# Keys asked for on another queue, and the opening split by heads: one change to a chunked delta rule with a maxout layer

## The chip, the cores and the metric

The kernel runs on one core of a Trainium2 chip. The time is device microseconds of one launch. Five engines work side by side, each on its own list of instructions in order: TensorE (PE in the profile; PEld is its loading of the stationary operand), VectorE (DVE), ScalarE (ACT), GpSimd (POOL) and SyncE (SP), which here only issues DMA transfers. POOL issues some too. An engine that reaches an instruction whose operand is not ready stands, and all behind it stand with it.

## The reference

Two parts, the second fed by the first. The first is a delta rule: for each of 4 batches and 8 heads a 48 x 48 state runs over 768 tokens.

```
k_n = k / (norm(k) + 1e-6)
for t in range(S):
    y[:, :, t] = q[:, :, t] @ state
    v_old = state^T k_t
    state = state + beta_t * outer(k_t, v_t - v_old)
x = y.transpose(0, 2, 1, 3).reshape(3072, 384)
```

The second is a maxout layer: `h = max(x @ w1, x @ w2, x @ w3)`, then `out = h @ w_out`, with w1 to w3 of 384 x 768 and w_out of 768 x 384. All operands are float32; the weights come as 64-bit floats, so that the kernel reads them as pairs of 32-bit words and puts float32 together itself.

## The kernel before, in words

**Tiles.** The 768 tokens are cut into 12 chunks of 64. A unit is one chunk for two of the four batches (one in each half of the 128 partitions), so chunk c has the units 2c and 2c + 1. Four units, that is two chunks, are a group, numbered m from 0; the third group has units 8 to 11 and chunks 4 and 5. `load_k(n)` and `load_q(n)` (L128 and L131; their transfers are issued in the helper `load`, L118) fetch a unit's keys and queries by two DMA transfers of 96 KB each; the keys of units 8 to 11 go into the buffers `kpad` that units 0 to 3 have used. `load_v(c)` fetches a chunk's values.

**What is made of a chunk.** Keys and queries are transposed by PE into `p_t` and copied to `kqt` (`turn`, L342 to L364). Gram products go into `p_g` (`gram`, L435): keys with keys give `at`, keys with queries give `pt`, masked on VectorE (L419). Within a chunk the delta rule needs the inverse of a triangular matrix. Its diagonal blocks are solved by column steps on VectorE (`solve`, the pairs L562 and L566), for a whole group at once; group 0's blocks return straight from VectorE's transpose to the tiles `ut` (L570 to L583), those of later groups go through DRAM (`y_d`, L588 and L597). For the first two groups (chunks 0 to 3) the solved blocks have 16 rows, and `halves_z` (PE `p_e`, copied to `zs`, L671 and L674), `halves_t` (VectorE transposes, L643 and L645) and `halves_u` (PE `p_f`, negated into `ut`, L678 and L680) join them to 32. Then `join_z` (`p_z`, L705 to L710), `turn_t1` (transposes L629 and L631) and `join_u` (`p_j`, negated, L719) join 32 to 64. With the inverse, `old_k` takes the state's part off the values (`p_k`), `new` makes u (`p_u`, copied at L769), `step` adds to the state (`p_s`, L787 and L794), `to_y` gives y (`p_y`, L806 to L810) and `to_x` transposes y into x (`p_x`, L820, copied at L870 to L873).

For chunk 0 `heads_of` cuts the heads into two halves of four, with a copy engine for each: ScalarE for the first, VectorE for the second. For later chunks there is one piece of eight heads, with ScalarE. Before the change `halves_u` and `join_u` do not use that engine: `negated` (L676) goes by `bb`, the half of the partitions.

**Norms and values.** `prep_values(c)` scales a chunk's values by the keys' norms on POOL (`scale`, L284), if that has not been done yet.

**Weights.** `fetch` (L213) asks for a piece of 384 KB on SP, into one of five buffers. A step of `weights` (called `conv`) scales a piece on ScalarE (L232, L233) and joins the piece before it, on VectorE (L243, L247) and POOL (L251). There are 24 pieces.

**The maxout layer.** `ffn(m)` treats the 512 tokens of group m. Each of its steps i is three matmuls into `p_h` (L922) in one of two PSUM banks, and a copy or maximum to `h`; at the end come four products into `p_o` (L954).

**Order.** The order of all instructions is written by hand; nothing is moved by a scheduler. The opening (chunk 0 and the start of chunk 1) is a straight list of calls from L990 to the start of `ffn(0)`. From there on the loop over the steps i of `ffn(0)` places the rest: `FIRST` (chunk 1 and the queries of group 0), `EARLY_LINKS` (chunks 2 and 3, and the transposes t and Gram products g of units 8 to 11: t0 stands at i = 11), and lines of its own for loads, weight steps and solving steps. Later groups go by `LINKS` in `ffn(1)` and on; there `p` means `prep_values`, and p1 stands at i = 5. The lines that matter here:

```
        if 7 <= i < 11:
            load_k(i + 1)
...
        if i in (22, 25):
            prep_values(4 + i // 25)
```

`load_k` without a second argument goes to SP's queue.

Of the kernel before, what the change touches and what calls it, by code (L numbers as in the profile page):

```python
# [21 lines left out]
def kernel(  # L22
# [495 lines left out]
    def solve(m):  # L518


        x = in_rows(xs[m])
        if m == 1:
            y_bl = in_wo(1)
        else:
            y_bl = work.tile([128, 2, HB * BL + HB], FP32, name="y_bl", bufs=1)
            if m:
                zero = kpad[0][:, 0:1, D : D + 1]
                nc.scalar.copy(y_bl, zero.to_broadcast(y_bl.shape))
            else:
                nc.gpsimd.memset(y_bl, 0.0)  # L530
        y = in_rows(y_bl)
        bl = small("bl", BL)
        norm(bl, diagonal(x), small("root_bl", BL), small("nt_bl", BL))
        if m:
            norms_of(m, bl)
        nc.vector.reciprocal(bl, bl)
        nc.vector.tensor_tensor(out=bl, in0=bl, in1=bl, op=ALU.mult)
        nc.vector.tensor_tensor(out=bl, in0=bl, in1=beta_bl[:, m] if m else beta_0, op=ALU.mult)
        (nc.scalar.copy if m else nc.gpsimd.tensor_copy)(diagonal(y), bl)
        if m < FINE:  # L540
            size, xv, yv = HB, in_blocks(xs[m]), in_blocks(y_bl)
            xb = xv[:, :, :, 0:HB]
            by = bl.rearrange("p (s i) -> p s i", i=HB)[:, :, None, :]
            by = by.to_broadcast([128, 2, HB, HB])
        else:
            size, xv, yv = BL, x[:, None], y[:, None]
            xb, by = x, bl[:, None, :].to_broadcast([128, BL, BL])
        nc.vector.tensor_tensor(out=xb, in0=xb, in1=by, op=ALU.mult)
        yield
        for j in range(size - 1):  # L550
            a, b = j + 1, size - 1 - j
            n = BL // size
            tmp = work.tile([128, 256], FP32, name="tmp")
            t_v = tmp[:, 0 : n * a * b].rearrange("p (s c i) -> p s c i", s=n, i=b)
            row, column, rest = (
                xv[:, :, j, None, j + 1 : size],
                yv[:, :, 0:a, j, None],
                yv[:, :, 0:a, j + 1 : size],
            )
            if n == 1:  # L560
                row, column, rest, t_v = (t[:, 0] for t in (row, column, rest, t_v))
            nc.vector.tensor_tensor(  # L562
                out=t_v, in0=row.to_broadcast(t_v.shape),
                in1=column.to_broadcast(t_v.shape), op=ALU.mult,
            )
            nc.vector.tensor_tensor(out=rest, in0=rest, in1=t_v, op=ALU.subtract)  # L566
            yield
        if m == 0:
            back = in_rows(xs[0])
            nc.vector.transpose(out=back, in_=y.rearrange("p c i -> p i c"))  # L570
            yield
            for cc in range(2):
                for i in range(4):
                    bb, half = divmod(i, 2)
                    r = block(bb, half)
                    to = ut[cc][r, :, :, BL * half : BL * (half + 1)].rearrange(
                        "p g h i -> p (g h) i"
                    )
                    of = back[r, :, 16 * cc : 16 * (cc + 1)].rearrange("p i x -> p x i")
                    if half:  # L580
                        nc.scalar.copy(to, of)
                    else:
                        (nc.gpsimd if cc else nc.vector).tensor_copy(to, of)  # L583
                yield
            return
        y_d = dram.tile([2, 2, B, H, BL, BL], FP32, name="y_d")
        for cc in range(2):
            nc.sync.dma_start(  # L588
                out=y_d[cc].rearrange("f b h i j -> (f b h) i j"),
                in_=y[64 * cc : 64 * (cc + 1)],  # L590
            )
        yield
        for cc in range(2):
            for half in range(2):
                for bb in range(2):
                    r0 = C * bb + BL * half
                    (one_queue if m or cc else both_queues)[bb].dma_start(  # L597
                        out=ut[cc][
                            r0 : r0 + BL, :, :, BL * half : BL * (half + 1)
                        ].rearrange("p g h i -> p (g h) i"),  # L600
                        in_=y_d[cc, half, 2 * bb : 2 * bb + 2].rearrange(
                            "b h c i -> c (b h) i"
                        ),
                    )
            yield
# [53 lines left out]
    def span(hs):  # L659
        return slice(hs[0], hs[-1] + 1)  # L660

    def halves_z(c):
        if c > 1:
            halves_t(c)
        at = [ats[2 * c + g] for g in range(2)]
        second = ut[c % NU].rearrange("p g h (f two x) -> p g h f two x", two=2, x=HB)
        for hs, p_v, copy in heads_of(c, "p_e", BL):
            for i, h in enumerate(hs):
                for bb, g in TILES:
                    r = rows(bb)  # L670
                    nc.tensor.matmul(  # L671
                        p_v[rows(bb ^ g), g, i], at[g][r, h], second[r, g, h, :, 1]
                    )
            copy(zs[c % NU][:, :, span(hs)], p_v)  # L674

    def negated(bb, to, of, c=0):  # L676
        if bb and c < 2:
            nc.vector.tensor_scalar_mul(to, of, -1.0)  # L678
        else:
            nc.scalar.mul(to, of, -1.0)  # L680

    def halves_u(c):
        t, z = fine.pop(c), zs[c % NU]
        for hs, p_v, _ in heads_of(c, "p_f", BL):
            for i, h in enumerate(hs):
                for bb, g in TILES:
                    r = rows(bb ^ g)
                    nc.tensor.matmul(p_v[rows(bb), g, i], t[g][r, h], z[r, g, h])
            for f in (0, 1):
                for bb in range(2):  # L690
                    r = block(bb, f, HB)
                    negated(
                        bb,
                        ut[c % NU][r, :, span(hs), BL * f + HB : BL * (f + 1)],
                        p_v[r, :, :, HB * f : HB * (f + 1)],
                    )

    def join_z(c):
        at = [ats.pop(2 * c + g) for g in range(2)]
        z, second = zs[c % NU], ut[c % NU][:, :, :, BL:C]  # L700
        for hs, p_v, _ in heads_of(c, "p_z", BL):
            for i, h in enumerate(hs):
                for bb, g in TILES:
# [1 line left out]
                    nc.tensor.matmul(  # L705
                        p_v[block(bb ^ g), g, i], at[g][r, h, 0:BL], second[r, g, h]
                    )
            nc.scalar.copy(z[block(0), :, span(hs)], p_v[block(0)])
            copy = nc.vector.tensor_copy if c < 2 else nc.scalar.copy
            copy(z[block(1), :, span(hs)], p_v[block(1)])  # L710

    def join_u(c):
        z, t = zs[c % NU], t1[c % NU]
        u12 = ut[c % NU][:, :, :, BL:C]
        for hs, p_v, _ in heads_of(c, "p_j", BL):
            for i, h in enumerate(hs):
                for bb, g in TILES:
                    r = block(bb ^ g)
                    nc.tensor.matmul(p_v[block(bb), g, i], t[r, g, h], z[r, g, h])  # L719
            for bb in range(2):  # L720
                negated(bb, u12[block(bb), :, span(hs)], p_v[block(bb)], c)


    xts, rhss, qss, us, yts = {}, {}, {}, {}, {}
# [33 lines left out]
    def new(c):  # L758
        rhs = rhss.pop(c)
        u = us[c] = both("u", D, 2)  # L760
        for hs, p_v, copy in heads_of(c, "p_u", D):
            for i, h in enumerate(hs):
                for bb, g in TILES:
# [3 lines left out]
                        rhs[rows(bb), g, h],  # L767
                    )
            copy(u[:, :, span(hs)], p_v)  # L769
        if c + NU < 2 * FINE:  # L770
            for bb in range(2):
                corner = ut[c % NU][block(bb), :, :, BL:C]
# [39 lines left out]
    def to_x(c):  # L812
# [1 line left out]
        if m not in xts:  # L814
            xts[m] = work.tile([128, KT, TOK], FP32, name="xt")
        y_f = yts.pop(c).rearrange("p g h d -> p g (h d)")
        p_x = ps_two("p_x")
        for g in range(2):
            for t in range(KT):
                nc.tensor.transpose(  # L820
                    p_x[:, g, t * 128 : (t + 1) * 128],
                    y_f[:, g, t::KT],
                    ident,
                )
        xt = xts[m][:, :, cc * 256 : (cc + 1) * 256].rearrange(
            "p t (g x) -> p g t x", g=2
        )
        copied(c, xt, p_x[:, :, 0 : KT * 128].rearrange("p g (t x) -> p g t x", t=KT))

    yds, yqs = {}, {}  # L830

# [24 lines left out]
    def turn_y(c):  # L856
# [6 lines left out]
            ),  # L863
            in_=yqs.pop(c).rearrange("p b (x t) -> p b t x", t=KT),
        )

    def copied(c, to, of):

        if c:
            nc.scalar.copy(to, of)  # L870
        else:
            nc.scalar.copy(to[:, 0], of[:, 0])
            nc.vector.tensor_copy(to[:, 1], of[:, 1])  # L873


    def less_first(f):
        part = (slice(None), slice(None), slice(f * 128, (f + 1) * 128))
# [167 lines left out]
        scale(c, nrm_0[:, c])  # L1045
    some(conv, 1)
    halves_u(0)
    turn_t1(0)
    join_z(0)
    masked(pts[0], by_par(pts[0]))  # L1050
    join_u(0)
    masked(pts[1], by_par(pts[1]))
    old_k(0)
    old_q(0)
    some(solving, 1)
    new(0)
    some(conv, 1)
    fetch(nc.sync)
    to_y(0)
    some(conv, 1)  # L1060
    fetch(nc.sync)
    halves_z(1)
    to_x(0)
    some(conv, 1)
    fetch(nc.sync)
    halves_t(1)
    load_q(4)
    load_v(2)
# [58 lines left out]
    for i, _ in enumerate(ffn(0)):  # L1127
# [7 lines left out]
            some(solving, (4, 2, 1)[i - 4])  # L1135
        if i in (5, 7):
            prep_values(i // 2)
        if 7 <= i < 11:
            load_k(i + 1)
        if i == 0:  # L1140
            load_v(3)
        if i == 12:
            load_q(11)
        if i in (10, 18):
# [3 lines left out]
        if i == 21:  # L1148
            solving = solve(2)
            some(solving, 1)  # L1150
        if i in (22, 25):
            prep_values(4 + i // 25)
        if 21 < i < 27:
            some(solving, 3)
        if i >= 27:
# [55 lines left out]
```

## Time and profile before

| what | value |
|---|---|
| median of 4 runs | 546.33 us (541.83 to 548.56) |
| the profiled execution | 546.7 us, span 545.0 us |
| PE busy | 507.4 us, 93% |
| DVE busy | 315.7 us, 58% |
| ACT busy | 155.3 us, 28% |
| POOL busy | 167.0 us, 31% |
| granted TensorE clock, mean | 0.952 |
| DMA | 53.49 MB, mean 98 GB/s |
| instruction queue | 63 packets, 1.03 MB |

The span is cut into 40 equal slices of 13.6 us; the page gives for each the busy share in tenths and, as PEclk, the clock that TensorE was granted in tenths of full speed:

```profile
PE   8558898889979999999998999999999999999996
...
PEclk9855799979989999999999999999999999999999
DMA  8872747973213494434375546483323401130011
```

From the thirteenth slice on PE is at 9 nearly throughout. What is below lies in the first twelve slices, up to 163 us; the clock is at a half in slices 3 and 4 (27 to 54 us), and for a part of several others up to slice 12.

"Issue" as the reason of a wait is time in which the engine waited for nothing that the profile shows. A wait for several events is put down to the last.

### The profile page before, as it was taken

What the parts mean: (1) busy time and instruction counts of PE and PEld (TensorE: products, weight loads), DVE (VectorE), ACT (ScalarE), POOL (GpSimd) and SP (SyncE); (2) the same over time, 40 slices, a digit from 0 to 9 for tenths busy, and PEclk for the clock granted to TensorE, in tenths of its full rate; (3) what the DMA queues carried; (4) which work ended last, traced back from release to release, by engine and by line L of the source; (5) the groups of instructions that cost most, each with busy time, mean ns of one, the idle gap of its engine ahead of it and who ended that gap; (6) DMA issues with size and microseconds to landing.
All of it is one profiled execution on the core that took longest, in us unless ns stands there. A gap on an engine that the chain in (4) does not pass through costs nothing.

```text
span 545.0 us, 18537 instructions
## 1 busy us (share of the span) xinstructions
PE 507.4 (93%) x8096; PEld 314.9 (58%) x8096; DVE 315.7 (58%) x701; ACT 155.3 (28%) x285; POOL 167.0 (31%) x279
## 2 busy tenths in 40 slices
PE   8558898889979999999998999999999999999996
PEld 7446677766535655556555556565565555654453
DVE  5886988665898544179854388671989313101100
ACT  4536364457310324220124210143201231010100
POOL 6315025122276073477065567141330000000000
PEclk9855799979989999999999999999999999999999
DMA  8872747973213494434375546483323401130011
GB/s 109 185 163 73 153 112 172 181 185 80 70 31 85 105 196 74 105 96 125 91 160 111 114 118 148 104 139 87 86 68 82 79 2 53 52 72 1 0 22 36
DMA packets 118848, 53.49 MB, mean 98 GB/s; under 512 B 100976, under 2 KB 113456, under 8 KB 118768
## 3 DMA queue, kind: packets, MB, share of 16 engines
q1 hardware_dynamic: 109872, 40.01, 33.9%
q0 software_dynamic: 6784, 11.92, 9.4%
q8 instruction: 63, 1.03, 0.8%
q10 hardware_dynamic: 2112, 0.39, 0.5%
q14 instruction: 17, 0.14, 0.1%
HBM read 39.17 MB, written 13.11 MB: 96 GB/s over the span
## 4 chain that ended last, share of the span: by engine, by line
PE 80%; DVE 11%; issue 3%; ACT 2%; DMA 2%; SPq 1%; POOL 0%; DVEq 0%; ACTq 0%; POOLq 0%
PE p_h L922 35%; PE p_o L954 24%; PE p_g L435 4%; PE p_m L902 2%; PE p_y L806 2%; PE p_k L736 2%; PE p_u L764 2%; DVE tmp L562 2%; DMA kpad<-in_k_dram 2%; PE p_j L719 2%; PE p_t L358 2%; PE p_q L736 1%; PE p_z L705 1%; PE p_s L787 1%; DVE y_bl L566 1%
## 5 line engine op out<-in xcount | busy, mean ns | idle before, releaser
L922 PE MATMUL p_h<-xt,w_sb 128*128 128x512 f32 (+1 forms) x522 | 222.9, 572 | 7.0 <-DVE h L936 3.6
L922 PEld LDWEIGHTS p_h<-xt,w_sb 128*128 128x128 f32 x522 | 98.0, 197 | 95.4 <-issue 88.4
L954 PE MATMUL p_o<-wo_sb,h 128*128 128x384 f32 x288 | 97.8, 489 | 0.0
L936 DVE TENSOR_TENSOR h<-h,p_h 128x512 f32<-128x512 f32 (+1 forms) x48 | 29.7, 618 | 96.6 <-PE p_h L922 96.5
L954 PEld LDWEIGHTS p_o<-wo_sb,h 128*128 128x128 f32 x288 | 53.7, 190 | 35.7 <-issue 0.5
L562 DVE TENSOR_TENSOR tmp<-x_bl,y_bl 128x31 f32<-128x31 f32 (+20 forms) x139 | 49.9, 359 | 4.1
L566 DVE TENSOR_TENSOR y_bl<-y_bl,tmp 128x31 f32<-128x31 f32 (+20 forms) x139 | 49.2, 354 | 4.8
L960 ACT COPY o_sb<-p_o 128x384 f32<-128x384 f32 x24 | 11.5, 480 | 141.7 <-PE p_o L954 135.7
L932 ACT ACTIVATE h<-p_h 128x512 f32<-128x512 f32 x30 | 17.9, 597 | 87.4 <-PE p_h L922 83.0
L954 PE MATMUL p_o<-w_sb,xt 128*128 128x384 f32 x120 | 42.0, 486 | 0.0
L393 POOL DMA_DIRECT2D turned<-in_q_dram x72 | 39.2, 552 | 3.1 <-POOL turned L388 3.1
L435 PE MATMUL p_g<-kqt 48*64 48x64 f32 (+1 forms) x1216 | 30.0, 246 | 10.8 <-ACT kqt L364 5.5
L251 POOL TENSOR_TENSOR w_sb<-mant,up 128x384 int32<-128x384 int32 x18 | 18.0, 999 | 59.5 <-DVE mant L247 51.0
L435 PEld LDWEIGHTS p_g<-kqt 48*64 48x64 f32 x1216 | 25.7, 145 | 18.1 <-issue 8.1
L954 PEld LDWEIGHTS p_o<-w_sb,xt 128*128 128x128 f32 x120 | 22.8, 190 | 15.9
L419 DVE TENSOR_TENSOR pt<-p_g,mask 128x512 f32<-128x512 f32 x22 | 15.2, 691 | 23.9 <-PE p_g L435 23.8
L284 POOL TENSOR_TENSOR v_t<-v_t,nrm 128x768 f32<-128x768 f32 x12 | 17.9, 1492 | 26.5 <-DVE nrm L263 13.5
L794 DVE TENSOR_TENSOR st<-st,p_s 48x768 f32<-48x768 f32 (+1 forms) x18 | 17.1, 951 | 15.0 <-PE p_s L787 14.8
L137 POOL DMA_DIRECT2D v_t<-in_v_dram x12 | 9.9, 830 | 38.9 <-PE p_u L764 38.9
L388 POOL MEMSET turned<- 128x96 f32 x18 | 3.3, 193 | 54.9 <-DVE kqt L409 34.7
L118 POOL DMA_DIRECT2D kpad<-in_k_dram x24 | 16.3, 688 | 11.5 <-PE p_s L787 11.5
L452 ACT COPY at<-p_g 128x512 f32<-128x512 f32 x21 | 12.3, 586 | 23.6 <-DVE pt L419 21.7
(150 smaller groups left out, 610.3 us busy)
## 6 DMA issues: line engine op xcount, KB each, us to landing
w_bits<-in_moe_w_dram SPq DMA_DIRECT2D x18, 384.0 KB, 4.8
out_dram<-o_sb SPq DMA_DIRECT2D x48, 96.0 KB, 2.2
turned<-in_q_dram POOLq DMA_DIRECT2D x72, 48.0 KB, 2.6
y_x<-y SPq DMA_DIRECT2D x16, 192.0 KB
qall<-y_x SPq DMA_DIRECT2D x32, 96.0 KB, 3.0
at_d<-at SPq DMA_DIRECT2D x80, 32.0 KB, 1.9
ut<-y_d SPq DMA_DIRECT2D x40, 64.0 KB, 2.7
qall<-in_q_dram SPq DMA_DIRECT2D x24, 96.0 KB, 4.2
```

Source lines behind the costliest of these rows:

```text
L251: nc.gpsimd.tensor_tensor(out=dst.bitcast(I32), in0=mant_v.bitcast(I32), in1=up_v, op=ALU.add)
L284: nc.gpsimd.tensor_tensor(out=vts[c], in0=vts[c], in1=nrm[:, :, :, None].to_broadcast([128, 2, H, D]), op=ALU.mult,)
L393: (queue, nc.gpsimd)[i].dma_start(out=t[p0 : p0 + 32, bb, at : at + NP * 2 * D].rearrange("p (j x) -> p j x", j=NP), in_=(k, q)[i][2 * bb ...
L435: nc.tensor.matmul(p_g[rows(bb ^ (g * i)), par, c0 : c0 + C * (1 + whole)], kq[:, 0], kq if whole else kq[:, i],)
L562: nc.vector.tensor_tensor(out=t_v, in0=row.to_broadcast(t_v.shape), in1=column.to_broadcast(t_v.shape), op=ALU.mult,)
L566: nc.vector.tensor_tensor(out=rest, in0=rest, in1=t_v, op=ALU.subtract)
L736: nc.tensor.matmul(p_b[rows(bb), par, c0 : c0 + D], kqt[g][dims(par), j, bb ^ g, i], st[dims(par), bb ^ g, g, j],)
L794: nc.vector.tensor_tensor(out=s_v[r], in0=s_v[r], in1=p_s[r, :, 0 : H * D], op=ALU.add)
L922: nc.tensor.matmul(p_h, w_sb[i][:, t, f * 128 : (f + 1) * 128], xt[:, t, lo : lo + w], start=(t == 0), stop=(t == KT - 1),)
L932: nc.scalar.activation(out=h, in_=p_h, func=mybir.ActivationFunctionType.Relu)
L936: nc.vector.tensor_tensor(out=h, in0=h, in1=p_h, op=ALU.max)
L954: nc.tensor.matmul(p_o, stays, moves, start=(n == 0), stop=(n == len(terms) - 1))
```

## The change

1. The keys of units 8 to 11. Before, `load_k(i + 1)` for 7 <= i < 11 on SP's queue. Now POOL issues units 8 and 9 at i = 1 and units 10 and 11 at i = 7.
2. The opening. In `solve`, of the four copies to chunk 0's `ut` three are VectorE's and one is ScalarE's (two and two before), and chunk 1's first-half copies go from POOL to VectorE. `halves_z` of chunk 0 copies both halves of the heads on ScalarE. `negated` takes the engine that `heads_of` gives: for chunk 0 ScalarE for the first four heads and VectorE for the last four, for later chunks ScalarE alone. `join_z` copies on ScalarE alone, also for chunks 0 and 1.
3. The order of the opening. `join_z(0)` stands ahead of `turn_t1(0)`, both masks behind `join_u(0)`, the weight step between `new(0)` and `to_y(0)` is gone from there and two stand behind `halves_z(1)`. `to_x(0)` stands ahead of `halves_z(1)`; its transposes go into a PSUM tile for each of the two g, each with its own copy (ScalarE, VectorE).
4. The zeroing of chunk 0's corner of `ut` (two ScalarE copies) leaves `new(0)` and stands at i = 0 of `ffn(0)`.
5. `prep_values(5)` at i = 25 is left out, so that p1 at i = 5 of `ffn(1)` does that scaling.

The diff, without the lines that only move a helper:

```
-                    if half:
+                    if half and (cc or bb):
                         nc.scalar.copy(to, of)
                     else:
-                        (nc.gpsimd if cc else nc.vector).tensor_copy(to, of)
+                        nc.vector.tensor_copy(to, of)
...
-            copy(zs[c % NU][:, :, span(hs)], p_v)
-
-    def negated(bb, to, of, c=0):
-        if bb and c < 2:
+            nc.scalar.copy(zs[c % NU][:, :, span(hs)], p_v)
+
+    def negated(copy, to, of):
+        if copy == nc.scalar.copy:
+            nc.scalar.mul(to, of, -1.0)
+        else:
             nc.vector.tensor_scalar_mul(to, of, -1.0)
-        else:
-            nc.scalar.mul(to, of, -1.0)
...
-            nc.scalar.copy(z[block(0), :, span(hs)], p_v[block(0)])
-            copy = nc.vector.tensor_copy if c < 2 else nc.scalar.copy
-            copy(z[block(1), :, span(hs)], p_v[block(1)])
+            for bb in range(2):
+                nc.scalar.copy(z[block(bb), :, span(hs)], p_v[block(bb)])
...
-                negated(bb, u12[block(bb), :, span(hs)], p_v[block(bb)], c)
+                negated(copy, u12[block(bb), :, span(hs)], p_v[block(bb)])
...
+        if c:
+            corner(c)
+
+    def corner(c):
         if c + NU < 2 * FINE:
...
+        for g, copy in enumerate((nc.scalar.copy, nc.vector.tensor_copy)):
+            p_x = ps_two("p_x")[:, 0]
+            turned_y(p_x, g)
+            copy(xt[:, g], p_x[:, 0 : KT * 128].rearrange("p (t x) -> p t x", t=KT))
...
     halves_u(0)
+    join_z(0)
     turn_t1(0)
-    join_z(0)
+    join_u(0)
     masked(pts[0], by_par(pts[0]))
-    join_u(0)
     masked(pts[1], by_par(pts[1]))
     old_k(0)
     old_q(0)
     some(solving, 1)
     new(0)
-    some(conv, 1)
-    fetch(nc.sync)
     to_y(0)
     some(conv, 1)
     fetch(nc.sync)
+    to_x(0)
     halves_z(1)
-    to_x(0)
-    some(conv, 1)
-    fetch(nc.sync)
+    for _ in range(2):
+        some(conv, 1)
+        fetch(nc.sync)
     halves_t(1)
...
-        if 7 <= i < 11:
-            load_k(i + 1)
+        if i in (1, 7):
+            for n in range(2):
+                load_k(8 + 2 * (i > 1) + n, (nc.gpsimd, nc.gpsimd))
         if i == 0:
             load_v(3)
+            corner(0)
...
-        if i in (22, 25):
-            prep_values(4 + i // 25)
+        if i == 22:
+            prep_values(4)
```

More of the change, by code (lines that the diff above doesn't have):

```diff
@@ L673, in halves_z @@
                     )
-            copy(zs[c % NU][:, :, span(hs)], p_v)
-    def negated(bb, to, of, c=0):
-        if bb and c < 2:
+            nc.scalar.copy(zs[c % NU][:, :, span(hs)], p_v)
[3 more added lines that the diff above has]
+        else:
             nc.vector.tensor_scalar_mul(to, of, -1.0)
-        else:
-            nc.scalar.mul(to, of, -1.0)
     def halves_u(c):
         t, z = fine.pop(c), zs[c % NU]
-        for hs, p_v, _ in heads_of(c, "p_f", BL):
+        for hs, p_v, copy in heads_of(c, "p_f", BL):
             for i, h in enumerate(hs):
@@ L692, in halves_u @@
                     negated(
-                        bb,
+                        copy,
                         ut[c % NU][r, :, span(hs), BL * f + HB : BL * (f + 1)],
@@ L714, in join_u @@
         u12 = ut[c % NU][:, :, :, BL:C]
-        for hs, p_v, _ in heads_of(c, "p_j", BL):
+        for hs, p_v, copy in heads_of(c, "p_j", BL):
             for i, h in enumerate(hs):
@@ L816, in to_x @@
         y_f = yts.pop(c).rearrange("p g h d -> p g (h d)")
[L817 to L824, printed above, removed]
         xt = xts[m][:, :, cc * 256 : (cc + 1) * 256].rearrange(
@@ L827, in to_x, with turned_y @@
         )
-        copied(c, xt, p_x[:, :, 0 : KT * 128].rearrange("p g (t x) -> p g t x", t=KT))
+        def turned_y(p_x, g):
+            for t in range(KT):
+                nc.tensor.transpose(
+                    p_x[:, t * 128 : (t + 1) * 128], y_f[:, g, t::KT], ident
+                )
+        if c:
+            p_x = ps_two("p_x")
+            for g in range(2):
+                turned_y(p_x[:, g], g)
+            nc.scalar.copy(
+                xt, p_x[:, :, 0 : KT * 128].rearrange("p g (t x) -> p g t x", t=KT)
+            )
+            return
+        for g, copy in enumerate((nc.scalar.copy, nc.vector.tensor_copy)):
+            p_x = ps_two("p_x")[:, 0]
+            turned_y(p_x, g)
+            copy(xt[:, g], p_x[:, 0 : KT * 128].rearrange("p (t x) -> p t x", t=KT))
     yds, yqs = {}, {}
@@ L865, in turn_y @@
         )
[L867 to L873, printed above, removed]
     def less_first(f):
```

## The prediction

> **What bounds the kernel now.** I read four views: the page's clock row, the table by stage, the waits of TensorE (PE) in the early part, the instructions in time order around each wait. First the stages: start and end, length, busy us of PE, weight loads, VectorE (DVE), ScalarE (ACT) and GpSimd (POOL), the granted clock, the DMA share.
>
> ```profile
> 28.40:55.70 27.30, 19.10 (x492) 16.19 (x496) 20.39 (x42) 14.44 (x29) 8.45 (x7) 0.50 0.56 130
> 101.06:113.70 12.64, 11.13 (x325) 9.43 (x325) 7.66 (x17) 6.28 (x13) 1.50 (x2) 1.00 0.90 184
> 113.70:120.60 6.90, 6.16 (x105) 4.97 (x106) 4.11 (x8) 3.98 (x9) 2.50 (x3) 0.51 0.62 118
> 156.20:159.20 3.00, 0.05 (x3) 0.07 (x1) 2.96 (x6) 0.00 (x0) 2.70 (x6) 0.82 0.06 16
> 158.10:165.00 6.90, 5.84 (x7) 2.50 (x8) 5.81 (x16) 0.00 (x0) 6.60 (x15) 0.51 0.28 74
> ```
>
> After 165 us PE hardly stops, so only what shortens PE's time before that shortens the kernel: its waits, and the stretches at half clock (0.50). The waits from 28 to 160 us (engine, line, what it waited for: total, times, longest):
>
> ```profile
> PE p_g L435 <- issue: 3.7, 2, 2.3
> PE p_h L922 <- DVE h L936: 3.6, 2, 2.9
> PE p_t L358 <- DMA kpad<-in_k_dram: 2.3, 1, 2.3
> PE p_g L435 <- DVE y L808: 1.6, 1, 1.6
> ...
> PE p_j L719 <- DVE z L710: 1.0, 1, 1.0
> ```
>
> The third line is what the change names. SP issues the keys of unit 8 at 95.28, behind its reads of the inverses (89.48 to 92.54), weights and queries, and PE stands until they land:
>
> ```profile
> 95.28 1.32 SPq L118 DMA_DIRECT2D kpad<-in_k_dram  x2
> ...
> 101.06 0.63 PE L358 MATMUL p_t<-ident,kpad 128*128 128x128 f32 x4 [2.31 <-DMA kpad<-in_k_dram]
> ...
> 114.44 1.14 PE L435 MATMUL p_g<-kqt 48*64 48x64 f32 x29 [2.25 <-issue]
> ```
>
> The last is a pause in the middle of one Gram product, where no operand is missing. The trace's packets on the instruction queue explain it: one starts at 111.53 and takes 1.22, PE resumes 1.69 after its end. The pauses at 41.17 and 62.28 likewise end 1.47 and 1.58 after packets that end at 40.28 and 62.19. PE has run out of instructions; the packets come late where DMA is busy (0.90 above).
>
> The wait of 2.95 us before 159.16:
>
> ```profile
> 153.40 0.90 DVE L562 TENSOR_TENSOR tmp<-x_bl,y_bl 128x60 f32<-128x60 f32 x1
> 154.18 2.91 POOL L284 TENSOR_TENSOR v_t<-v_t,nrm 128x768 f32<-128x768 f32 x2
> 154.34 1.40 DVE L566 TENSOR_TENSOR y_bl<-y_bl,tmp 128x60 f32<-128x60 f32 x1
> ...
> 155.77 1.43 DVE L562 TENSOR_TENSOR tmp<-x_bl,y_bl 128x87 f32<-128x87 f32 x1
> ...
> 159.16 8.26 PE L922 MATMUL p_h<-xt,w_sb 128*128 128x512 f32 x12 [2.95 <-DVE h L936]
> ```
>
> While POOL scales two chunks of values, DVE steps that take 0.19 just before and 0.25 just after take 1.4; the maximum that frees PE's PSUM bank is queued behind them.
>
> **Third group's keys.** SP loses eight loads (0.62 each, 5 us of issue). POOL gains four issues after its fifth weight join and four after the scaling of chunk 3. A keys issue on POOL takes 684 ns (24 rows, at most 722), so 4 x 0.684 = 2.74. The fifth join ends at 70.27, the sixth starts at 73.81: 2.74 fits, and the piece it makes is needed by p_h only at 75.53, so cost 0. The second four run from about 92.3 to 95.0 and push the next join (92.80) by 2.2; its piece belongs to columns that p_h reaches after 127, and ACT's next scaling, which needs the buffer, started at 96.74 against a join now ending at 96.0: 0. Neither set waits, since the state updates that read the old keys ended at 57.3 and 81.2. Bounds: an issue stretched as DVE's were (by 1.18) takes 1.86, four 7.4, and the sixth join starts 3.3 late (+3.3); below nothing, POOL's two ut copies (2.62) are gone (0). I take 0, the row of the same issue. Unit 8 would have landed by 80 and its queries, issued at 88, by 93, so PE goes on at 98.75: **-2.3**. Next late would be unit 9's queries (issued 93.32, wanted at 102.6) or the T transposes (end 101.5, wanted at 104.9): neither is. Ends: -2.3 and 0.
>
> [...]
>
> **The pause at 112.19.** The eight loads of 96 KB (SP, 95.28 to 105.0) leave this stretch, four to 70 us and four to 92, and v_t's next load, issued behind them at 105.05, goes some 5 us sooner; so the packet that PE lacks meets queues less full. Its delay is the estimate: unchanged (0) to gone (-2.25). I take **-1.3**, over half, because weights (107.42) and queries (108.71) still lie just ahead of it.
>
> **Scaling of chunk 5** leaves i = 25 and falls to the next group's loop, on POOL near 199 us, where PE stands on nothing and chunk 5's keys are subtracted at 239.85. One of the two L284 goes: 1.43 - 0.25 = **-1.2**. Ends 0 and -1.5 (its whole duration).
>
> **Opening.** Part by part, by rows.
> - Of chunk 0's copies to ut, ACT had two (1.06 each, to 32.95), DVE two (0.60). Now DVE has three, to 32.62: p_e starts 0.3 sooner.
> - halves_u(0): eight pieces alternate, each engine waiting for the other, 36.31 to 38.65. By halves: four on ACT (0.28) and four on DVE (0.30) side by side, to about 38.1: -0.5.
> - join_z(0) all on ACT (4 x 0.36, to 39.6) and DVE's transposes ahead (to 39.5): p_j could start at 39.55 for 40.54. But the instruction pause inside p_j ended at 41.75 by a packet delayed by loads (DMA 0.94 there) that do not move. If it stays, the second 1.0 is lost.
> - DVE then does, in order, two negations (0.84), two masks (1.38), two ut copies taken from POOL (1.20), and only then half of u: 46.7 for 45.53. p_y ends at 47.8 (47.61 before).
> - p_x (1.55) goes ahead of p_e (1.9), whose work now covers the copies of x: p_h starts at 51.95 for 52.02. That is all the reorder is worth.
> - New wait: DVE's third join needs ACT's scaling, which now stands behind the copy of z, which waits for p_e. 51.95 + 0.59 + 0.45, then 0.95 of DVE, then transposes 2.15: they end at 56.15, and p_f is queued behind them: 56.2 for 54.85, **+1.35**. Without the pause it would be 54.15, **-0.7**. Behind DVE wait the norm chain (3.0) and PE's p_z, so this goes through to about 84 us.
> - There, PE waits 1.57 for y and 0.53 for a weight join, both from a DVE that is full. DVE gives ACT 2 x 0.43 + 0.69 + 0.69 = 2.24 of chunk 1's pieces and copies; ACT has idle stretches of 4 us to take them. The zeroing of the corner (2 x 0.61, ACT) moves to i = 0; z's copies then end at 65.9 for 63.71, hidden by PE's pause to 63.77 and the product after it.
> So the lateness is mostly eaten. I take **-0.2**, between ends -1.0 and +1.4. For chunks 2 and 3 the pieces go to ACT alone (four of 0.38, as long as the alternation took): 0.
>
> **Clock.** p_h at half clock took 8.26 for 12 against 5.35 at full clock: 2.9 per stretch of 6.8 us; at 113.7 the sum of p_g, p_h, p_z and p_t gives 2.8. Both follow a pause that this change shortens. I take half of one and a sixth of the other, **-1.9**; ends: both, -5.7, and +3.4 (the opening's half clock, released at 55.7 after p_h without a break, lasts one stretch more because p_h is now followed by a wait).
>
> [...]
>
> **Sum.** The profiled execution took 546.7 (span 545.0 and 1.7 around it), 0.4 over the median of 546.33. 546.7 - 2.3 - 1.3 - 1.2 - 0.2 - 1.9 = 539.8; less exactly, against the median, I say 540.
>
> **Rivals.**
> 1. Only the two plain waits go (keys, scaling); the instruction pause stays at its packet and the clock falls as before. For: the pause is a matter of DMA queues, of which weights and queries remain. Against: DMA share falls. 546.7 - 3.5 = 543.2.
> 2. The keys' wait is replaced: PE reaches the next missing instructions 2.3 earlier and stands there instead, so the change does not bring what it says. For: the packet of 98.34 ended at 99.47, and 1.6 later is 101.07, the very time PE resumed; against: by count of instructions that packet serves work some 140 further on. 546.7 - 1.2 = 545.5.
> 3. Slower: the half clock of the opening lasts. PE was granted full clock at 55.72 after p_h and p_f without a gap; with p_f 1.35 later, the release slips by two windows, to 62.5 (the trace's half-clock stretches, 6.83 and 27.3, are multiples of 3.41). Work of 5.54 busy us there doubles, +5.5, p_f's own +1.35, less 3.5 for the plain waits: 550. It decides from one window (2.7) on, with the pause at 112 unchanged. Against: DVE's norm chain (54.86 to 57.86) holds PE there anyway, and the 2.1 of waiting near 80 eats part.
>
> **How the numbers follow.** Forecast 540: 0.47 (its own range 537 to 542.5); rival 1: 0.25; rival 2: 0.11; rival 3: 0.11; more clock won back, 536: 0.06. Range 536 to 547: it leaves out the lower part of the last and most of rival 3. A measurement of this kernel tells from no change only about 1%, 5.5 us: faster means under 540.9. From the forecast 0.36 and from the last 0.06 lie below: 0.42; slower (over 551.8) is a third of rival 3 and a rest for unknowns: 0.07; same 0.51.
>
> **What would show it.** Right: no wait for kpad at unit 8's p_t; POOL keys issues near 70 at 0.68; one L284 near 150 and the tmp after it at 0.25; p_g of unit 9 unbroken; ACT and DVE pieces of p_f overlapping near 37. Wrong: p_f of chunk 1 starting over 1.5 later than 54.85, the first join after 70 later than 74.5, an "issue" wait near 100, or half clock after 59.

## The result, and the profile after

| kernel | median | lowest to highest | runs |
|---|---|---|---|
| before | 543.63 us | 538.62 to 550.62 | 55 |
| after | 541.12 us | 537.24 to 548.31 | 34 |

The ratio after to before is 0.9957, with a 95% interval from 0.9938 to 0.9976: about 2.3 us faster, under 1%. The 546.33 that the prediction started from was the median of four runs; 55 runs give 543.63. The profiled execution of before (546.7) was thus 3 us above the middle, and this matters for what follows. The profiled execution of after took 543.1, with a span of 541.0 us and a mean clock of 0.955.

Line numbers shift: L922 and L936 of before are L926 and L940 of after. First the table by stage of after, columns as in the prediction:

```profile
28.60:62.70 34.10, 26.14 (x598) 22.33 (x598) 25.28 (x59) 16.78 (x39) 6.12 (x6) 0.50 0.54 123
91.40:103.70 12.30, 9.29 (x264) 7.73 (x256) 9.29 (x16) 4.25 (x7) 5.78 (x8) 1.00 1.13 189
103.70:110.50 6.80, 5.37 (x56) 4.78 (x56) 0.00 (x0) 3.40 (x7) 0.00 (x0) 0.50 0.94 145
153.30:156.30 3.00, 1.23 (x66) 1.06 (x65) 2.93 (x7) 0.59 (x1) 2.71 (x7) 1.00 0.07 16
156.30:161.60 5.30, 5.30 (x12) 2.16 (x12) 4.96 (x14) 0.00 (x0) 5.01 (x11) 1.00 0.33 84
```

The clock column (third from the end) shows three changes: the opening's half clock lasts to 62.70 instead of 55.70, there is a new stretch at half clock from 103.70, and the one behind 158 is gone. The waits of TensorE from 28 to 170 us:

```profile
PE p_e L671 <- DVE ut L583: 5.9, 2, 5.7
PE p_f L688 <- issue: 4.4, 1, 4.4
PE p_h L926 <- DVE h L940: 2.4, 2, 1.8
PE p_u L763 <- issue: 1.5, 1, 1.5
PE p_j L718 <- issue: 1.4, 1, 1.4
PE p_g L435 <- DVE y L811: 1.2, 1, 1.2
...
```

The wait for kpad (2.3) is gone, and so is p_g's pause for instructions. The first line is the wait for the first blocks of chunk 0, which before has too (6.1). The second is a pause for instructions that before did not have, of 4.4 us in chunk 2's p_f. In order of time:

```profile
41.71 0.74 PE L718 MATMUL p_j<-z,t 32*32 32x32 f32 x35 [1.42 <-issue]
...
56.04 1.80 PE L688 MATMUL p_f<-z,t 64*64 64x32 f32 x57 [0.31 <-DVE t L645]
...
69.86 2.76 POOL L118 DMA_DIRECT2D kpad<-in_k_dram  x4
73.22 1.15 POOL L251 TENSOR_TENSOR w_sb<-mant,up 128x384 int32<-128x384 int32 x1 [0.60 <-DVE mant L247]
...
97.35 0.66 PE L358 MATMUL p_t<-ident,kpad 128*128 128x128 f32 x4
...
105.13 1.48 PE L688 MATMUL p_f<-z,t 64*64 64x32 f32 x42 [4.44 <-issue]
...
152.49 1.48 POOL L284 TENSOR_TENSOR v_t<-v_t,nrm 128x768 f32<-128x768 f32 x1
...
154.08 0.25 DVE L562 TENSOR_TENSOR tmp<-x_bl,y_bl 128x87 f32<-128x87 f32 x1
...
156.29 5.39 PE L926 MATMUL p_h<-xt,w_sb 128*128 128x512 f32 x12 [1.77 <-DVE h L940]
```

Unit 8's transposes start at 97.35 with nothing in front of them (101.06 before), so TensorE is 3.7 ahead there. At 105.13 it has just stood for 4.44 us. The trace's packet of instructions starts at 101.77 and ends at 103.33; TensorE goes on 1.80 later. The last three lines are the scaling: one L284 instead of two, VectorE's step behind it at 0.25, the wait of p_h 1.77 instead of 2.95, and its twelve matmuls at full clock.

### The profile page after: what moved, and what is told of

The parts are those of the page before. It is cut to its first block, busy times and chain, and to the rows that moved or that the text cites. A ratio compares the mean times of both kernels' runs of the same rounds, so it can differ in the third digit from the quotient of the medians.

```text
span 541.0 us, 18549 instructions
## 1 busy us (share of the span) xinstructions
PE 507.4 (94%) x8096; PEld 316.2 (58%) x8096; DVE 313.1 (58%) x693; ACT 158.7 (29%) x295; POOL 170.0 (31%) x285
## 4 chain that ended last, share of the span: by engine, by line
PE 83%; DVE 11%; issue 3%; ACT 1%; DMA 1%; SPq 0%; POOL 0%; DVEq 0%; ACTq 0%; POOLq 0%
PE p_h L926 35%; PE p_o L958 25%; PE p_g L435 4%; PE p_m L906 2%; PE p_y L809 2%; PE p_t L358 2%; PE p_k L735 2%; PE p_u L763 2%; DVE tmp L562 2%; PE p_q L735 2%; PE p_s L790 2%; PE p_j L718 1%; PE p_z L705 1%; PE p_f L688 1%; DVE y_bl L566 1%
## 5 line engine op out<-in xcount | busy, mean ns | idle before, releaser
L926 PE MATMUL p_h<-xt,w_sb 128*128 128x512 f32 (+1 forms) x522 | 220.8, 568 | 2.5 <-DVE h L940 2.4
L926 PEld LDWEIGHTS p_h<-xt,w_sb 128*128 128x128 f32 x522 | 97.6, 196 | 89.3 <-issue 82.9
L940 DVE TENSOR_TENSOR h<-h,p_h 128x512 f32<-128x512 f32 (+1 forms) x48 | 29.7, 618 | 103.3 <-PE p_h L926 102.3
L562 DVE TENSOR_TENSOR tmp<-x_bl,y_bl 128x31 f32<-128x31 f32 (+20 forms) x139 | 50.6, 364 | 4.1
L566 DVE TENSOR_TENSOR y_bl<-y_bl,tmp 128x31 f32<-128x31 f32 (+20 forms) x139 | 49.4, 355 | 4.8
L936 ACT ACTIVATE h<-p_h 128x512 f32<-128x512 f32 x30 | 17.9, 598 | 88.8 <-PE p_h L926 84.5
L118 POOL DMA_DIRECT2D kpad<-in_k_dram x32 | 21.9, 691 | 12.8 <-PE p_s L790 12.8
L284 POOL TENSOR_TENSOR v_t<-v_t,nrm 128x768 f32<-128x768 f32 x12 | 17.9, 1493 | 24.8 <-DVE nrm L263 13.4
L763 PEld LDWEIGHTS p_u<-v_t,ut 64*64 64x64 f32 x768 | 13.6, 141 | 9.8 <-issue 8.7
```

What stands on the lines that cost most here:

```text
L118: queues[bb].dma_start(out=dst[rows(bb ^ g), :, 0:D], in_=src[2 * bb + g, :, c * C : (c + 1) * C, :].rearrange("h p d -> p h d"),)
L284: nc.gpsimd.tensor_tensor(out=vts[c], in0=vts[c], in1=nrm[:, :, :, None].to_broadcast([128, 2, H, D]), op=ALU.mult,)
L562: nc.vector.tensor_tensor(out=t_v, in0=row.to_broadcast(t_v.shape), in1=column.to_broadcast(t_v.shape), op=ALU.mult,)
L763: nc.tensor.matmul(p_v[rows(bb ^ g), g, i], ut[c % NU][rows(bb), g, h], rhs[rows(bb), g, h],)
L926: nc.tensor.matmul(p_h, w_sb[i][:, t, f * 128 : (f + 1) * 128], xt[:, t, lo : lo + w], start=(t == 0), stop=(t == KT - 1),)
L940: nc.vector.tensor_tensor(out=h, in0=h, in1=p_h, op=ALU.max)
```

## The experiments

Three theories were in play. A: the keys' gain is given back at one place, the new pause near 100, since SP, freed of the keys, issues its other loads back to back. B: the opening eats it, above all by its longer half clock. C came after the first four runs: between 75 and 115 us loads and instruction packets meet differently in each execution, and a stall at one place hides the next.

The table holds, for one profiled execution of each kernel, from the lines of the timeline: the time from the first p_e to the p_g near 82 (the opening), unit 8's wait for kpad, the sum of all of TensorE's waits from 84 to 122, the time from the start of the last p_s to that of the twelve p_h, and from there to p_y (5.3 is full clock, 8.2 half).

| kernel | ratio, 95% interval | opening | kpad | waits 84-122 | p_s to p_h | p_h to p_y |
|---|---|---|---|---|---|---|
| before | | 51.5 | 2.3 | 4.9 | 4.10 | 8.19 |
| before_again | 1.0002, 0.9966 to 1.0037 | 51.3 | 2.5 | 4.7 | 4.09 | 5.32 |
| keys_only | 1.0016, 0.9981 to 1.0050 | 51.0 | 0 | 2.7 | 4.09 | 7.02 |
| opening_only | 1.0029, 0.9994 to 1.0065 | 50.3 | 2.4 | 4.2 | 4.09 | 8.19 |
| scale_only | 0.9876, 0.9831 to 0.9920 | 51.8 | 0 | 1.9 | 2.92 | 5.32 |
| scale_again | 0.9935, 0.9899 to 0.9971 | 51.3 | 2.5 | 5.3 | 2.91 | 7.02 |
| scale_v4_late | 0.9963, 0.9931 to 0.9994 | 49.9 | 1.6 | 3.6 | 2.92 | 5.32 |
| no_opening | 0.9965, 0.9930 to 1.0001 | 51.1 | 0 | 4.1 | 2.92 | 5.31 |
| no_keys | 0.9968, 0.9938 to 0.9998 | 50.4 | 0.4 | 1.7 | 2.91 | 5.32 |
| after | 0.9957, 0.9938 to 0.9976 | 50.3 | 0 | 4.4 | 2.91 | 5.32 |
| after_again | 0.9933, 0.9907 to 0.9959 | 50.5 | 0 | 2.6 | 2.91 | 5.32 |
| after_v4_late | 0.9934, 0.9900 to 0.9968 | 50.6 | 0 | 2.3 | 2.91 | 5.32 |
| both_late | 0.9957, 0.9928 to 0.9985 | 50.9 | 2.9 | 4.2 | 1.74 | 5.32 |
| after_both_late | 0.9959, 0.9924 to 0.9994 | 52.2 | 0 | 4.6 | 1.74 | 5.31 |

### keys_only: the keys alone

```
-        if 7 <= i < 11:
-            load_k(i + 1)
+        if i in (1, 7):
+            for n in range(2):
+                load_k(8 + 2 * (i > 1) + n, (nc.gpsimd, nc.gpsimd))
```

> The kernel before with the change of the keys alone (four issues on GpSimd at i = 1 and four at i = 7, none on SP at i = 7 to 10). Theory A (the gain of the keys is given back as an instruction pause, because SP, freed of the keys, issues weights, queries and v_t back to back from 95 to 102): the wait for kpad at unit 8's p_t (2.31) is gone, and one 'issue' pause of 3 to 5 us stands near 100 to 105 in its place, the one of 2.25 near 112 is gone; 0 to -2 us against the kernel before. Theory B (the opening of the changed kernel eats what the keys bring): no new pause near 100, the clock falls one stretch less, and the time is 3 to 5 us below the kernel before.

The wait for kpad is gone and the time is not: median 545.55, and the interval excludes more than 1 us of gain. The pause near 112 shrank to 0.34. What stands now is a wait for something else, 1.65 us one product earlier:

```profile
95.02 0.30 PE L671 MATMUL p_e<-ut,at 64*64 64x32 f32 x4
...
96.97 1.28 PE L671 MATMUL p_e<-ut,at 64*64 64x32 f32 x48 [1.65 <-DMA ut<-y_d]
```

`ut<-y_d` is SP's read of the solved blocks of chunks 2 and 3. SP issues the part for chunk 3 from 89.47 to 92.81, POOL its second four keys from 90.15 to 92.88: the two now run side by side. That this makes the read late is likely: TensorE goes on 5.8 us after SP issued the last part of it (91.15), while in both_late below, with the keys on SP, it reaches the same products as early (92.31 and 94.82), 4.1 after that issue (90.75), and does not wait. Theory A named the right outcome, but the wrong place and the wrong kind of wait; B expected 3 to 5 us and fell.

### scale_only and scale_again: the scaling alone

```
-        if i in (22, 25):
-            prep_values(4 + i // 25)
+        if i == 22:
+            prep_values(4)
```

> The kernel before without the scaling of chunk 5 at i = 25. One L284 near 154 instead of two, the tmp after it at 0.25 instead of 1.43, the wait of p_h for DVE's h at 159 down from 2.95 to about 1.8. Theory A: the stretch at half clock from 158.1 to 164.9 goes too, p_h's twelve matmuls at 5.4 instead of 8.26, together -1.2 - 2.9 = -4.1 in its profiled execution; theory B: the clock falls after 1.8 as after 2.95, and only -1.2 is gained.

> The kernel before without the scaling of chunk 5 at i = 25, a second time, since its first six runs gave 0.9876 and the four kernels that hold it with something more gave 0.9934 to 0.9968. Theory C (the scaling is the only part that moves the time: 1.2 of wait in every execution, 2.87 of clock in those where the longer wait is followed by half clock, 3 of the 4 seen): 1.2 + 0.65 x 2.87 = 3.1, a ratio of 0.994, within 0.992 to 0.997. Rival (keys and opening each cost about 2 us when the scaling is already gone): 0.9876 again, under 0.991. By both, 2.9 from p_s to p_h in the profile and 5.3 for the twelve matmuls after it.

All of the gain, and more than theory B had: medians 538.86 (6 runs) and 540.63 (12 runs). In both the time from p_s to p_h fell from 4.1 to 2.9, and the first shows the wait and the full clock that theory A had:

```profile
152.99 5.39 PE L922 MATMUL p_h<-xt,w_sb 128*128 128x512 f32 x12 [1.77 <-DVE h L936]
```

The second, in which theory C was right about the size, shows that a wait of 1.76 can be followed by half clock too:

```profile
157.32 7.08 PE L922 MATMUL p_h<-xt,w_sb 128*128 128x512 f32 x12 [1.76 <-DVE h L936]
```

### opening_only: the opening alone

```
-        if i in (1, 7):
-            for n in range(2):
-                load_k(8 + 2 * (i > 1) + n, (nc.gpsimd, nc.gpsimd))
+        if 7 <= i < 11:
+            load_k(i + 1)
...
-        if i == 22:
-            prep_values(4)
+        if i in (22, 25):
+            prep_values(4 + i // 25)
```

(against the changed kernel)

> The changed kernel with the keys back on SP at i = 7 to 10 and the scaling of chunk 5 back at i = 25: the changes of the opening alone. Theory A: p_f of chunk 1 near 56.0 as in the changed kernel, half clock to 62.7 or 55.9 by execution, the lateness mostly absorbed by the waits near 80; within 1.5 us of the kernel before. Theory B: the opening costs 2 to 4 us, because the longer half clock goes through to the end.

Median 545.08, within 1.5 us of before, as A had it; B's 4 us are outside the interval, its 2 us are not. The stage itself is not longer: 50.3 against 51.1 on average over the eight executions with the old opening.

### after_v4_late: fewer loads around the late packet

```
-        if i in (10, 18):
+        if i in (14, 18):
             load_v(4 + i // 18)
```

> The changed kernel with load_v(4) at i = 14 instead of i = 10, which takes the two v_t issues of 99.45 out of the burst on SP's queue that stands around the late instruction packet (101.77 to 103.33). Theory A (the pause of 4.44 us in p_f of chunk 2 comes of that burst): the packet starts earlier, the pause near 105 shrinks to under 2, the half clock after it goes, and the time is 2 to 5 us below the changed kernel's. Theory B (the packet is late for another cause, the inverses' reads or the count of instructions): the pause stays at about 4, and the time is within 1 us of the changed kernel's.

The pause of 4.44 was gone, and in its place stood two waits of p_e for `ut<-y_d`, 2.3 together. The median was 540.11. This looked like theory A until the changed kernel itself was profiled again.

### before_again and after_again: the two kernels once more

> The kernel before, unchanged, profiled a second time. Theory A (the wait for kpad of 2.3 and the pause of 2.25 are in every execution, and something in the changed kernel takes their gain back): both stand again, within 0.5 us, and the stretch from 165 to the end takes 379 us again. Theory C (where PE stands between 75 and 115 is a matter of the execution: loads and instruction packets meet differently each time, and a pause at one place hides the wait at the next): one of the two is missing or under 1 us, another pause stands in its place, and the stretch after 165 differs by over 1 us. By both, the wait of 2.95 for DVE's h and the half clock after it stand again.

> The changed kernel, unchanged, profiled a second time. Theory A (SP's loads, back to back since the keys left its queue, always delay the packet at p_f of chunk 2): a pause of 3 to 5 us near 103 again. Theory C (it is a matter of the execution): that pause is missing or under 2, the half clock after it with it; from p_g near 82 to p_s near 153 it takes 68 to 69 instead of 70.8. By both, 2.9 from p_s to p_h, 5.3 for its twelve, and 0.9957 for the time.

The waits of before_again from 28 to 170 us:

```profile
...
PE p_h L922 <- DVE h L936: 3.6, 2, 2.9
PE p_g L435 <- issue: 3.1, 2, 1.6
PE p_t L358 <- DMA kpad<-in_k_dram: 2.5, 1, 2.5
...
```

The wait for DVE's h stands as before, and so does the wait for kpad: A was nearer here, since C had it or the pause missing. But p_g's pause near 112 is 1.6 instead of 2.25, and the half clock behind h is not there (5.32), which neither foresaw. The stretch from p_y to the end took 379.5 where the first execution took 377.6. And after_again:

```profile
...
PE p_g L435 <- issue: 3.1, 3, 1.9
PE p_h L926 <- DVE h L940: 2.4, 2, 1.8
PE p_j L718 <- issue: 2.0, 1, 2.0
PE p_q L735 <- issue: 1.5, 1, 1.5
...
```

No pause for instructions in p_f at all: theory A, by which it stands in every execution, falls. But the pause is not a matter of one execution either. At the same matmul of p_f it stands in three of the six executions with GpSimd's keys (4.44 in after, 3.07 in after_both_late, 1.43 in no_opening), and in one of the eight with SP's, at 0.33. In after_both_late:

```profile
107.25 1.47 PE L688 MATMUL p_f<-z,t 64*64 64x32 f32 x42 [3.07 <-issue]
```

So the change of the keys seems to make it likelier; six executions against eight do not settle it. From p_g near 82 to p_s it took 68.6 instead of 70.8, inside what C expected, and the median, 539.44, is the same as that of after_v4_late: the thinner burst of loads had done nothing to the time that can be measured.

### no_opening and no_keys: one part left out

no_opening is the two edits of keys_only and scale_only in the kernel before; no_keys is the changed kernel with

```
-        if i in (1, 7):
-            for n in range(2):
-                load_k(8 + 2 * (i > 1) + n, (nc.gpsimd, nc.gpsimd))
+        if 7 <= i < 11:
+            load_k(i + 1)
```

> The kernel before with the keys on GpSimd and without the scaling of chunk 5 at i = 25: the changed kernel without its opening. If the parts add up as measured alone (keys 1.0016, scaling 0.9876), the ratio is about 0.989; if the keys bring what the prediction took (2.3 and 1.3 and some clock), 0.981 to 0.984. Half clock ends near 56, and a pause of 1 to 4 us near 100 by theory A; by theory C it may be anywhere from 75 to 115, or missing.

> The changed kernel with the keys back on SP at i = 7 to 10: the opening and the scaling. If the parts add up as measured alone (opening 1.0029, scaling 0.9876), the ratio is about 0.9905, and the changed kernel (0.9957) loses by its keys; if the keys bring what the prediction took, it is 0.999 to 1.002. A wait for kpad of up to 2.4 at unit 8's p_t unless PE is held up before.

Medians 541.30 and 541.88. Both miss what was expected of sums with 0.9876, which later proved to be the far end of the scaling's own spread. Neither differs from the whole change: with the keys or without, with the opening or without, the ratio is 0.993 to 0.997 wherever the scaling is gone, but for the six runs of scale_only. A least-squares fit over the 222 runs of the kernels that differ by these three parts alone gives, with 95% intervals: scaling -3.7 us (0.9 either way), keys +0.4 (0.9), opening +0.6 (0.9).

### scale_v4_late: the load moved in the kernel without the second scaling

The edits of scale_only and of after_v4_late in the kernel before.

> The kernel before without the scaling of chunk 5 at i = 25 and with load_v(4) at i = 14 instead of 10. Theory A: two v_t loads fewer around the packets of 105 to 113, so no pause over 1 us between 95 and 120, 0.5 to 2 us below the scaling alone (0.9876). Theory C: the pauses move, the sum stays; within 1 us of the scaling alone. Either way it should lie below the changed kernel.

Median 541.04; no pause for instructions longer than 0.74 between 84 and 122, two waits for kpad of 1.6 together instead. The load's place is worth nothing that can be measured here either.

### both_late and after_both_late: can the other scaling go as well?

```
-        if i in (22, 25):
-            prep_values(4 + i // 25)
+        if i == 28:
+            prep_values(4)
```

(in the kernel before; in the changed kernel its `if i == 22:` becomes `if i == 28:`)

> The kernel before with the scaling of chunk 5 gone from i = 25 and that of chunk 4 moved from i = 22 to i = 28, where GpSimd has a group of query loads to issue first (4.4 us): no L284 beside DVE's steps ahead of the maximum that p_h waits for. Theory: the two steps stretched to 0.90 and 1.40 take 0.2 each, the maximum comes 1.9 sooner, p_s to p_h falls from 2.91 to about 1.1 and the time by 1 to 2 us below the scaling of chunk 5 alone. Rival: the scaling, now near 154, stretches the DVE steps there (0.32) instead and the next maximum, at 157.7, is late by as much, so p_h gains and p_o loses: no change.

> The changed kernel with the scaling of chunk 4 moved from i = 22 to i = 28 in the same way. Theory: p_s to p_h falls from 2.91 to about 1.1, and the time lies 1 to 2 us below the changed kernel (ratio near 0.993); rival: the next maximum is late by as much and nothing changes (0.9957).

On the time the rival was right. In both_late:

```profile
153.96 5.39 PE L922 MATMUL p_h<-xt,w_sb 128*128 128x512 f32 x12 [0.59 <-DVE h L936]
...
155.36 2.60 DVE L566 TENSOR_TENSOR y_bl<-y_bl,tmp 128x156 f32<-128x156 f32 x1
156.28 1.49 POOL L284 TENSOR_TENSOR v_t<-v_t,nrm 128x768 f32<-128x768 f32 x1
...
161.79 3.46 PE L954 MATMUL p_o<-wo_sb,h 128*128 128x384 f32 x10 [1.36 <-DVE h L936]
...
165.80 0.88 PE L954 MATMUL p_o<-wo_sb,h 128*128 128x384 f32 x2 [0.54 <-DVE h L936]
```

p_h's wait fell to 0.59 and p_s to p_h to 1.74, 1.18 less again; the theory had about 1.1, for it took both long VectorE steps for the scaling's work, and the one of 0.90 stayed (150.56 to 151.46, beside a weight join of GpSimd from 150.34 to 151.38). And the VectorE step that was 0.32 in scale_only took 2.60 with GpSimd's scaling beside it, the next maxima are late, and p_o waits 1.36 and 0.54: 1.9 back for 1.2 gained. Medians 541.91 and 542.03. No version was found that beats the kernel with the one scaling gone.

## Why the prediction was right or wrong

The time (540 for 541.12), the range and the likeliest class held. Part of that is luck: of the forecast's 6.3 us below 546.33, 2.3 are in the measured ratio, 2.7 are that 546.33 was high, and the rest did not come. It is luck too that the terms were wrong in opposite directions: the scaling brought more than the sum gave it, the keys and the pause behind them nothing that can be measured.

- **Scaling of chunk 5: right mechanism, size too small.** The sum had -1.2 for the wait and, under Clock, a share of 2.9. The wait is exact: 4.09 to 2.91 is 1.18, in every one of the twelve executions with one or both scalings in their old place. The clock was mis-sized: p_h to p_y is 7.18 on average over the four executions with the wait of 2.95 and 5.53 over the eight with 1.77, so 1.65. Together 2.8; the fit says 3.7, 0.9 either way. The prediction took half of one stretch and a sixth of another and does not say which was which: half of 2.9 would have been nearly right, a sixth is 1.2 too little. Done in the later loop, the scaling costs nothing that shows: from p_y to the end it takes 379.1 on average over those eight executions and 380.0 over the four. The clock fell after the wait of 2.95 in three of the four executions and after that of 1.76 in one of the eight.
- **Keys: the step "-2.3" failed.** The wait went, and unit 8 started 3.7 sooner in the profile of after. "Next late would be unit 9's queries or the T transposes: neither is" was wrong. Next late were the read of the inverses that p_e needs (1.7, 1.0 and 2.3 us in keys_only, no_opening and after_v4_late) or the packet of instructions that p_f needs (4.4, 3.1 and 1.4 in after, after_both_late and no_opening). The means of TensorE's waits from 84 to 122 show the exchange:

| keys on | kpad | inverses | p_f's packet | p_g's packet near 112 | other | sum |
|---|---|---|---|---|---|---|
| SP (eight executions) | 1.8 | 0 | 0.0 | 0.9 | 1.0 | 3.8 |
| GpSimd (six) | 0 | 0.8 | 1.5 | 0.4 | 0.8 | 3.5 |

This is rival 2, which had 0.11, with a wider reach than it was given: the argument of the 140 instructions held for one place, and the stall went to others. The transfers are dense in that stretch: 162 to 171 GB/s from 84 to 106 in all fourteen, with the keys early or late, and DMA shares of 0.78 to 1.00. In scale_only and no_keys, with SP's keys and hardly a wait for them, TensorE had been slowed before (half clock from 83.0 and from 91.3) and came when they had landed. That the transfers' volume is the cause is argued from these rows; no run took loads out, and that the rate is a limit is not shown (scale_only moved 186 GB/s from 106 to 122).

- **GpSimd's four issues: 0, right.** They took 2.76 beside VectorE, and the sixth join started at 73.22. VectorE ran six TENSOR_TENSOR steps, one TENSOR_SCALAR and one SCALAR_TENSOR_TENSOR beside these four.
- **The pause at 112.19: -1.3 failed,** with its share of the clock. The term priced a pause of one execution. At the same matmul of p_g TensorE stood for 2.25, 1.63, 1.15 and 0.88 in four executions with SP's keys and 0.61 or less in the other four; with GpSimd's keys for 1.70 in one of six and 0.34 or less in the others. So the mean fell by 0.5, and p_f's packet took more than that back.
- **Opening: -0.2, in line with the runs.** p_f of chunk 1 started at 56.04 (56.2 foretold), p_j's pause ended at 41.71 (41.75), the first p_h at 51.73 (51.95). The stage takes 50.7 on average over six executions and 51.1 over the eight with the old opening; the fit's 0.6 (0.9 either way) does not tell the opening from no change.
- **Rival 3: the longer half clock, yes; 550, no.** With the new opening it lasted to 61 or beyond in three of six executions, with the old one in none of eight. But with the old opening a second stretch at half clock follows between 59 and 70 in seven of the eight (62.5 to 69.4 in before), and with the new one it is shorter or missing. From 25 to 70 us the clock is at a half for 33.0 us on average with the new opening and for 32.4 with the old: a window moved, none was added.
- **The signs.** An "issue" wait of over 1 us between 95 and 110 came in three of six executions with GpSimd's keys, so as a sign it needs several profiles. "Half clock after 59" was badly put, since before itself had a stretch from 62.5.

## What to carry to other kernels

Profile a kernel twice before pricing its stalls: the wait for VectorE's maximum came back to 0.01 us in every execution of the same order (p_s to p_h 4.09, 2.91 or 1.74); waits for transfers, pauses for instructions and stretches of half clock did not, and their mean over executions is their price. Where the transfers are dense (162 to 171 GB/s from 84 to 106 here), an earlier request for one of them can move the wait to the next: the wait for kpad, 1.8 on average, went, and the sum of the waits fell by 0.3. So ask what would be late next among all transfers of that stretch, the instructions' own packets included. A stall that ends in half clock cost more than its length: behind the wait of 2.95 in before, p_h to p_y took 8.19 where it takes 5.32 at full clock. Price both.

## What the runs showed of the hardware

- In before and in after all starts and ends of half-clock stretches within the span lie on one grid of 3.413 us, to 0.001 us (28.41 to 55.72 in before is 8 steps of it, 28.58 to 62.72 in after 10); counted from the start of the span, the two grids lie 0.17 us apart. The same stall was followed by half clock in some executions and not in others: that of 2.95 us in 3 of 4 (p_h to p_y 8.19, 8.19 and 7.02, against 5.32), that of 1.77 in 1 of 8 (7.02), and a pause for instructions of 1.3 to 2.6 us that ends between 279 and 292, in 7 of 10 executions (all but after_again, scale_again, both_late and after_both_late; the next five or six p_h took 4.07 to 5.49, against 2.41 for five in the other three). What decides it was not shown.
- The instruction queue moved 63 packets of 16 KB in the span of before and in that of after, beside 16192 matmuls and weight loads: one for every 257 of them. That these packets hold TensorE's instructions is argued from this count and from the pauses: the seven of over 0.8 us for instructions in the two executions ended 1.4 to 1.8 us after the end of a packet. When the packet that ended at 103.33 in after, the fifteenth, started, TensorE had started 171 instructions more than at the start of the fifteenth in before (4033 and 3862), and it stood for 4.44. In after_again, the same kernel, it did not stand for instructions there; in before the wait behind that packet, of 2.31 to 101.06, is put down to kpad.
- In before and in after, eleven of the solving steps (L562, L566) began while a GpSimd TENSOR_TENSOR had over 0.1 us to go. Ten ended 0.07 to 0.15 us after it, with 0.51 to 1.32 us of it left when they began; the eleventh, begun 0.01 us after its start, took 0.28. A step that began before it can end with it too: that of 2.60 us in both_late ran from 155.36 to 157.96, and the scaling's record from 156.28 to 157.77.
